# Expert products of an attention and feed-forward kernel cut in halves and, behind value passes, in column strips; four of seven products of a quad in one PSUM bank

## The chip, the cores and the metric

The kernel runs on one core of a Trainium2 chip, in one launch. The metric is the device time in microseconds (us), the median of several executions. TensorE is the engine for matrix products (PE in the profile, PEld for its weight loads), VectorE is DVE, ScalarE is ACT, GpSimd is POOL, and SyncE is SP, which issues the stores here.

## What is computed

Softmax attention over 8 batches, 12 heads, 448 tokens and 64 elements a head, then a feed-forward layer with SiLU on the 3,584 tokens:

```python
scores = scale * np.matmul(q, k.transpose(0, 1, 3, 2))
scores = scores - np.max(scores, axis=-1, keepdims=True)
attn = np.exp(scores)
attn = attn / (np.sum(attn, axis=-1, keepdims=True) + 1e-09)
attn_out = np.matmul(attn, v)
x = attn_out.transpose(0, 2, 1, 3).reshape(B * S, H * D)   # 3584 x 768
h = x @ w_in                                               # 768 x 2048
g = h * (1.0 / (1.0 + np.exp(-h)))
out = g @ w_out                                            # 2048 x 768
```

## The kernel before, in words

**The attention.** A unit is one batch with a group of four heads (`units`, line 801; batch 0 is cut in two pieces of 224 tokens, `PIECES`). For each unit TensorE makes scores (`score`, line 336), with 64 elements of a head as two passes of 32 rows: four heads stand one below the other in the array as tiles of 32 rows by 128 columns. ScalarE takes the exponential of each pair of banks (`expo`, line 373). Then come three passes through `attend`, each with output strips of 128 rows by 32 columns, four heads side by side: part 0 sums the exponentials (`attend_sums`, line 415, for a pair of units), parts 1 and 2 are the value passes (line 399), each for half of a head's elements. Two units share one chunk of keys; its strips have 64 rows and end each value pass of a pair of units. VectorE divides (`norm`, line 482) and leaves x transposed.

**The feed-forward layer.** Up to batch 5, `ffn1` (line 496) makes a group of six products of 128x128 weights by 448 tokens (224 in the pieces of batch 0) in one PSUM bank. ScalarE takes a tanh (line 507) and VectorE makes g from it (`gate`, line 543). The second layer runs on quads of two by two blocks: `product` (line 704), with seven products of eight matmuls with 384 columns in place of eight, on sums and differences of blocks of g (`combine_g`, line 694) and of `w_out` (`combine_w`, line 533). Four banks take them, two products in three of the banks (`BANK`, line 696); `take_3` to `take_7` read the banks, three by ScalarE and six additions by VectorE per quad. Quad 0 is done without the trick, by `plain` (line 718). The first layer of the last two batches (`PB`) uses the same kind of seven products, over two batches and two halves of the weights (`pair_product`, line 632), eight times (f = 0 to 7), with two copies on ScalarE and five additions on VectorE each (`pair_copy`, `pair_add`), and then four SiLUs on ScalarE (line 670). The outputs lie in `ost` buffers and are stored by SP, the last ones in turn by SP and ScalarE (`store`, line 762).

**The order.** The order of every engine is fixed when the kernel is built. A planner (`Order`, lines 78 to 162, and the loop from line 1496) keeps a clock for each engine with an estimated cost for each operation, rings for the buffers (`m_ring` for four PSUM banks, `s_ring` for two pairs of score banks, `ost_ring` for output buffers), and whenever TensorE is free it takes scores if they are ready and due (`PACE`), else a value pass, else the first ready entry of the list `moe` (groups of `ffn1`, quad products, pair products). `on_pe` adds `SWITCH`, 0.094, when the mode of the array (full, rows, cols and the two kinds of 64-row or 64-column rest) differs from that before. Where nothing is ready early on, products of zeros fill (line 1491).

```python
    def on_pe(self, op, mode):
        gap = SWITCH if mode != self.mode else 0.0
        self.mode = mode
        op.busy += gap
        self.start(op)
...
            elif moe_i is not None:
                if av is not None and av <= od.now - 0:
                    run_av()
                else:
                    moe.pop(moe_i)[2]()
                ran = True
```

Of the kernel before, what the change touches and what calls it, by code (L numbers as in the profile page):

```python
# [17 lines left out]
PE_OUT = 0.20  # L18
# [147 lines left out]
def kernel(  # L166
# [36 lines left out]
    SHY = 0.5  # L203
    FAR = (NT * B // 4 - 3, NT * B // 4 - 1)
# [4 lines left out]
    NSG, NTMP, NOST = 3, 3, 4  # L209
# [213 lines left out]
    def attend(ns, part):  # L423
        made = []
        lone = len(ns) == 1
        if part == 0 and not lone:
            attend_sums(ns)
            return
        for n in ns:
            a = ps.tile([128, 512], FP32, name=f"a_{n}_{part}", tag="m", bufs=4)  # L430
            made.append(a)
            acc[(n, part)] = a
            for c in range(NCH if lone else NCH - 1):
                for h in range(HG):
                    attend_mm(
                        a, n, part, c, h, 0, rows_of(n, c), E[(n, c // per_burst(n))],
                        c == 0, lone and c == NCH - 1,
                    )
        if not lone:
            for h in range(HG):  # L440
                for i, n in enumerate(ns):
                    attend_mm(
                        made[i], n, part, 3, h, 64 * i, 64 * (i + 1), E[(ns[0], 3)],
                        False, True,
                    )

# [43 lines left out]

    h_t, th_t, o_t = {}, {}, {}

    def ffn1(b, f, t0, t1):
        h = ps.tile([128, 512], FP32, name=f"h_{b}_{f}_{t0}", tag="m", bufs=4)
        for cc in range(NDC):
            nc.tensor.matmul(  # L496
                out=h[:, 0 : t1 - t0],
                lhsT=w_in_t[:, cc, 128 * f : 128 * (f + 1)],
                rhs=x3(b, cc)[:, cc % 3, t0:t1],
                start=(cc == 0),  # L500
                stop=(cc == NDC - 1),
            )
        h_t[(b, f, t0)] = h
# [13 lines left out]
    W_ = {m: const.tile([128, HF, OH], FP16, name=f"D{m}") for m in (1, 4, 6)}  # L517
# [5 lines left out]
    W_[3], W_[7], W_[5], W_[2] = B_[0, 1], B_[1, 0], B_[1, 1], B_[0, 0]  # L523

    def combine_w(m, f0, f1):
        i0, i1, op = {
            1: ((0, 0), (1, 1), ALU.add),
            4: ((1, 0), (0, 0), ALU.subtract),
            6: ((0, 0), (0, 1), ALU.add),
            3: ((0, 1), (1, 1), ALU.subtract),  # L530
            7: ((1, 0), (1, 1), ALU.add),
        }[m]
        nc.vector.tensor_tensor(
            out=W_[m][:, f0:f1], in0=B_[i0][:, f0:f1], in1=B_[i1][:, f0:f1], op=op
        )
# [75 lines left out]
    PBANK = {1: "A", 2: "A", 6: "B", 5: "C", 3: "C", 7: "D", 4: "D"}  # L611

    def pair_product(f, m):
        if m in (1, 5):
            pp_t[(f, PBANK[m])] = ps.tile(
                [128, 512], FP32, name=f"f_{f}_{m}", tag="m", bufs=4
            )[:, 0:S]
        elif m == 6:
            two = ps.tile([128, 2, 512], FP32, name=f"f_{f}_{m}", tag="s", bufs=2)
            pp_t[(f, "B")], pp_t[(f, "D")] = two[:, 0, 0:S], two[:, 1, 0:S]  # L620
# [10 lines left out]
        for c in range(3):  # L631
# [4 lines left out]
                start=(c == 0 and m in (1, 6, 5, 7)),  # L636
# [4 lines left out]
    def pair_tmp(f, name):  # L641
# [4 lines left out]
            "v": ("T", NT_, [128, HG, S], FP16),  # L646
        }[name]
        t = sb.tile(shape, dt, name=f"{name}_{f}", tag=tag, bufs=n)
        if len(shape) == 5:
            t = t.rearrange("p c x i e -> p (c x i e)")  # L650
        elif len(shape) == 3:
            t = t.rearrange("p h s -> p (h s)")
# [6 lines left out]
    def pair_add(f, to, x, y):  # L659
        x = pp_t[(f, x)] if x in "BCD" else pf_t[(f, x)]  # L660
        y = pf_t[(f, y)]
        out = pf_t[(f, to)] if (f, to) in pf_t else pair_tmp(f, to)
        nc.vector.tensor_tensor(out=out, in0=x, in1=y, op=ALU.add)
# [13 lines left out]
    S_t, tmp_t, ost_t, pr_t = {}, {}, {}, {}  # L677

    def combine_g(qd, m, f0, f1):
        a, b = 2 * qd, 2 * qd + 1  # L680
        x, y, op = {
            5: (rows(a, 0), rows(a, 1), ALU.add),
            2: (rows(b, 0), rows(b, 1), ALU.add),
            1: (rows(a, 0), rows(b, 1), ALU.add),
            6: (rows(b, 0), rows(a, 0), ALU.subtract),
            7: (rows(a, 1), rows(b, 1), ALU.subtract),
        }[m]
        if m > 5:
            dst = x
        else:  # L690
            if (qd, m) not in S_t:
                S_t[(qd, m)] = sb.tile([128, HF, 128], FP16, name=f"S_{qd}_{m}", tag="S", bufs=NSG)
            dst = S_t[(qd, m)]
        nc.vector.tensor_tensor(out=dst[:, f0:f1], in0=x[:, f0:f1], in1=y[:, f0:f1], op=op)  # L694

    BANK = {3: 3, 5: 3, 4: 4, 2: 4, 1: 1, 7: 1, 6: 6}

    def product(qd, m):
        w = {3: rows(2 * qd, 0), 4: rows(2 * qd + 1, 1), 6: rows(2 * qd + 1, 0), 7: rows(2 * qd, 1)}
        w = w[m] if m in w else S_t[(qd, m)]  # L700
        if BANK[m] == m:
            pr_t[(qd, m)] = ps.tile([128, 512], FP32, name=f"p_{qd}_{m}", tag="m", bufs=4)
        for f in range(HF):
            nc.tensor.matmul(  # L704
                out=pr_t[(qd, BANK[m])][:, 0:OH],
                lhsT=w[:, f, :],
                rhs=W_[m][:, f, :],
                start=(f == 0 and BANK[m] == m),
                stop=(f == HF - 1),
                skip_group_check=True,  # L710
            )


    def plain(t, j, f0, f1):
        if f0 == 0:
            pr_t[("o", t, j)] = ps.tile([128, 512], FP32, name=f"o_{t}_{j}", tag="m", bufs=4)
        for f in range(f0, f1):
            nc.tensor.matmul(  # L718
                out=pr_t[("o", t, j)][:, 0:OH],
                lhsT=rows(t, f // HF)[:, f % HF, :],  # L720
                rhs=B_[f // HF, j][:, f % HF, :],
                start=(f == 0),
                stop=(f == NFF - 1),
                skip_group_check=True,
            )
# [7 lines left out]

    def tmp(qd, name):
        tmp_t[(qd, name)] = sb.tile([128, OH], FP32, name=f"{name}_{qd}", tag="tmp", bufs=NTMP)
        return tmp_t[(qd, name)]
# [28 lines left out]
    def add(out, a, b, op=ALU.add):  # L765
        nc.vector.tensor_tensor(out=out, in0=a, in1=b, op=op)  # L766


    def take_3(qd):
        nc.scalar.copy(out=tmp(qd, "s"), in_=bank(qd, 3))  # L770

    def take_4(qd):
        add(tmp_t[(qd, "s")], bank(qd, 4), tmp_t[(qd, "s")])

    def take_5(qd):
        nc.scalar.copy(out=ost(qd, 0, 1), in_=bank(qd, 3))  # L776
        store(qd, 0, 1)

    def take_2(qd):
        nc.scalar.copy(out=ost(qd, 1, 0), in_=bank(qd, 4))  # L780
        store(qd, 1, 0)

    def take_1(qd):
        add(tmp(qd, "m"), bank(qd, 1), tmp_t[(qd, "s")])

    def less_12(qd):
        add(tmp_t[(qd, "s")], tmp_t[(qd, "s")], ost_t[(qd, 0, 1)], ALU.subtract)

    def less_21(qd):
        add(tmp_t[(qd, "m")], tmp_t[(qd, "m")], ost_t[(qd, 1, 0)], ALU.subtract)  # L790

    def take_6(qd):
        add(ost(qd, 1, 1), bank(qd, 6), tmp_t[(qd, "m")])
        store(qd, 1, 1)

    def take_7(qd):
        add(ost(qd, 0, 0), bank(qd, 1), tmp_t[(qd, "s")])
        store(qd, 0, 0)
# [113 lines left out]
    sg_ring, tmp_ring, ost_ring = Ring(NSG), Ring(NTMP), Ring(NOST)  # L912
    far_ring = Ring(NX3)
    STORE = 3.0
    pr_op, sg_op, w_op, plain_op = {}, {}, {2: [], 5: []}, {}
    inv_op, norm_op = [], []
    quads = []

    def queue_ffn1(b, g0, g1):
        t0, t1 = 32 * g0, 32 * g1  # L920
        for f in range(NFF) if b == 0 else [x for f in range(HF) for x in (f, f + HF)]:

            def run(f=f):
                op = Op("PE", NDC * mm(t1 - t0), lambda: ffn1(b, f, t0, t1), tail=PE_OUT)
# [4 lines left out]
                od.on_pe(op, "full")  # L929
# [14 lines left out]
            def deps(f=f):  # L944
# [3 lines left out]
                for qd in range(NT * B // 4) if u else ():  # L948
                    if any(t // NT == u - 1 and (r or t % NT < 4) for t in (2 * qd, 2 * qd + 1)):
# [3 lines left out]
                            else [pr_op.get((qd, m)) for m in (3, 4, 6, 7)]  # L953
# [56 lines left out]
    def queue_pair_f(f, xs):  # L1010
        done, lo = {}, f // 4 * 4

        def free(r):
            made = []
            for qd in range(NT * B // 4):
                for t in (2 * qd, 2 * qd + 1):
                    if t // NT == PB // 2 - 1 and t % NT < (4, NT - 1)[r]:
                        made += [pr_op.get((qd, m)) for m in (3, 4, 6, 7)]
# [10 lines left out]
        def queue(m):  # L1029
            rings = {  # L1030
                1: ((rq_ring, 1),),
                6: ((s_ring, 1), (kt_ring, 1), (t_ring, 1)),
                5: ((rk_ring, 1),),
            }.get(m, ())
            ms = (6, 7) if m == 6 else (m,)

            def run():
                op = Op(
                    "PE",
                    3 * len(ms) * mm(S),  # L1040
                    lambda: [pair_product(f, x) for x in ms],
                    tail=PE_OUT,
                )
                if m in (1, 5):
# [7 lines left out]
                elif m == 6:  # L1052
                    read("u", "DVE", lambda: pair_add(f, "u", "B", "p"), [op, done["p"]])
                    read("v", "DVE", lambda: pair_add(f, "v", "D", "u"), [op, done["u"]])
                elif m == 5:
                    read("q", "ACT", lambda: pair_copy(f, "q", "C"), [op], None, -3)
                    read("22", "DVE", lambda: pair_add(f, "v", "q", "v"), [done["v"], done["q"]], rk_ring.give)
                    gate_of(1, 1, "v", [done["22"]], t_ring.give)
                elif m == 2:
                    gate_of(0, 0, "A", [op], m_ring.give)  # L1060
                elif m == 3:
                    read("12", "DVE", lambda: pair_add(f, "p", "C", "u"), [op, done["u"]], m_ring.give)
                    gate_of(1, 0, "p", [done["12"]], rq_ring.give)
# [520 lines left out]
```

## Time and profile before

| What | Value |
|---|---|
| three timed runs | 396.12 us median, 396.03 to 396.42 |
| span of the profiled execution, first to last instruction | 394.4 us; the median of the runs is 1.7 above it |
| first matmul, last matmul | 1.0 us and 389.5 us after the span's start |
| 0 to 25 us: PE busy | 22.6 us (loads land, zeros fill) |
| 25 to 300 us: attention and both layers mixed | PE 274.6 of 275 us, DVE 228.6, ACT 189.7 |
| 311 to 349 us: pair products | PE 38.0 of 38 us, DVE 33.0, ACT 21.2 |
| 349 us to the end: last four quads | PE 40.9 of 45 us, DVE 30.5, ACT 10.5 |
| loads and stores | 45.6 MB read, 11.0 MB written |

Busy time of PE is modelled at its end (a matmul of 448 columns shows 352 ns, but the next starts 189 ns later), so the distance from one start to the next is what a matmul takes from the engine. Four strips that stand in different rows or columns of the array start 2 to 4 ns apart and run side by side; in what follows they are one group, and a slot is one group or one full matmul.

### The profile page before, as it was taken

How to read it: one execution, taken by the hardware profiler on the slowest of the kernel's cores; microseconds unless marked ns; L12 is line 12 of the kernel's file. 1: busy time of each engine (PE TensorE's matmuls, PEld its weight loads, DVE VectorE, ACT ScalarE, POOL GpSimd, SP SyncE). 2: the span in 40 equal slices, each digit the busy share in tenths (PEclk: the TensorE clock that was granted, in tenths of full speed). 3: DMA queues.
4: the chain of work that ended last, by engine and by line, in shares of the span. 5: the costliest groups of instructions: out<-in, count | busy, mean ns of one | idle time of the engine just before them, and what ended most of it. 6: DMA issues, size and time to landing. Idle time of an engine off the chain costs nothing.

```text
span 394.4 us, 9273 instructions
## 1 busy us (share of the span) xinstructions
PE 386.5 (98%) x3679; PEld 199.0 (50%) x3679; DVE 311.3 (79%) x653; ACT 243.2 (62%) x378; POOL 83.6 (21%) x153
## 2 busy tenths in 40 slices
PE   7999999999999999999999999999999999999995
PEld 6667764443444444554444444344444555556663
DVE  2466676999999697896888786988879898787863
ACT  4988885696863868626868429686593227872110
POOL 6632546315004242500051221120000000000000
PEclk9999999999999999999999999999999999999999
DMA  7999999919034863582145751531100131001334
GB/s 113 205 210 210 166 179 164 175 36 141 1 76 88 142 95 47 75 158 71 25 49 81 139 109 46 71 48 42 42 1 2 40 87 35 2 1 42 80 82 121
DMA packets 35356, 34.44 MB, mean 87 GB/s; under 512 B 11376, under 2 KB 33776, under 8 KB 35312
## 3 DMA queue, kind: packets, MB, share of 16 engines
q0 software_dynamic: 24784, 22.82, 39.2%
q1 hardware_dynamic: 9952, 10.33, 9.6%
q10 hardware_dynamic: 576, 0.69, 0.6%
q8 instruction: 29, 0.48, 0.5%
q14 instruction: 15, 0.12, 0.1%
HBM read 45.61 MB, written 11.01 MB: 144 GB/s over the span
## 4 chain that ended last, share of the span: by engine, by line
PE 94%; DMA 3%; DVE 1%; ACT 1%; POOL 0%; issue 0%; POOLq 0%
PE p L704 29%; PE h L496 29%; PE s L336 12%; PE a L399 10%; PE f L632 8%; PE o L718 3%; DMA rq<-in_q_dram 3%; PE a L415 2%; PE z L1491 1%; ACT E L373 0%; DVE S L694 0%; POOL rk L249 0%; DVE rq L323 0%; DVE rdn L466 0%; DVE ost L766 0%
## 5 line engine op out<-in xcount | busy, mean ns | idle before, releaser
L373 ACT ACTIVATE E<-s 128x896 f16<-128x896 f32 (+1 forms) x172 | 150.0, 915 | 48.6 <-PE s L336 47.5
L496 PE MATMUL h<-xT,w_in_t 128*128 128x448 f16 (+1 forms) x672 | 118.6, 327 | 0.0
L496 PEld LDWEIGHTS <-w_in_t 128*128 128x128 f16 x672 | 61.2, 98 | 54.0 <-issue 18.0
L507 ACT ACTIVATE th<-h 128x448 f16<-128x448 f32 (+1 forms) x112 | 54.3, 495 | 31.4 <-PE h L496 22.5
L543 DVE SCALAR_TENSOR_TENSOR G<-th,h 128x448 f16<-128x448 f16 (+2 forms) x112 | 55.1, 507 | 15.3 <-ACT th L507 13.3
L270 POOL DMA_DIRECT2D V<-in_v_dram x88 | 48.5, 568 | 56.5 <-PE a L399 42.7
L336 PE MATMUL s<-rq,KT 32*128 32x448 f16 (+4 forms) x768 | 50.9, 337 | 1.4 <-DVE rq L323 0.9
L704 PEld LDWEIGHTS <-G 128*128 128x128 f16 x384 | 36.5, 98 | 28.1 <-issue 4.4
L704 PEld LDWEIGHTS <-S 128*128 128x128 f16 x312 | 29.3, 98 | 23.9 <-issue 5.2
L399 PE MATMUL a<-E,V 128*32 128x448 f16 (+3 forms) x864 | 40.4, 335 | 0.0
L255 POOL DMA_DIRECT2D rq<-in_q_dram x27 | 15.1, 560 | 113.0 <-PE s L336 82.9
L704 PE MATMUL p<-D,G 128*128 128x384 f16 x208 | 37.6, 326 | 0.0
L704 PE MATMUL p<-w_out_t,S 128*128 128x384 f16 x208 | 37.2, 326 | 0.1
L482 DVE SCALAR_TENSOR_TENSOR xT<-a,rdn 128x448 f16<-128x448 f32 (+1 forms) x54 | 28.7, 565 | 7.4 <-PE a L399 6.5
L336 PEld LDWEIGHTS <-KT 32*128 32x128 f16 (+2 forms) x864 | 17.5, 98 | 29.6 <-issue 25.9
L704 PE MATMUL p<-w_out_t,G 128*128 128x384 f16 x176 | 31.9, 326 | 0.0
L399 PEld LDWEIGHTS <-V 128*32 128x32 f16 (+2 forms) x864 | 18.2, 95 | 22.4 <-issue 14.7
L384 DVE TENSOR_TENSOR T<-T,E 128x1792 f16<-128x1792 f16 x20 | 21.8, 1089 | 8.0 <-ACT E L373 7.9
L694 DVE TENSOR_TENSOR S<-G 128x512 f16<-128x512 f16 x70 | 25.3, 414 | 3.2 <-PE p L704 3.0
L384 DVE TENSOR_TENSOR T<-E,E 128x1792 f16<-128x1792 f16 x20 | 21.6, 1082 | 5.6 <-ACT E L373 5.6
L776 ACT COPY ost<-p 128x384 f32<-128x384 f32 x13 | 6.2, 480 | 27.4 <-PE p L704 22.6
L305 DVE STREAM_TRANSPOSE KT<-rk 128x256 f32<-128x256 f32 (+3 forms) x48 | 16.6, 384 | 7.0 <-DMA rk<-in_k_dram 6.2
(74 smaller groups left out, 370.2 us busy)
## 6 DMA issues: line engine op xcount, KB each, us to landing
out_dram<-ost SPq DMA_DIRECT2D x194, 48.0 KB, 1.7
rk<-in_k_dram POOLq DMA_DIRECT2D x24, 224.0 KB, 5.9
rq<-in_q_dram POOLq DMA_DIRECT2D x21, 224.0 KB, 5.2
w_in_t<-in_moe_w_in_dram POOLq DMA_DIRECT2D x6, 512.0 KB, 11.2
w_out_t<-in_moe_w_out_dram POOLq DMA_DIRECT2D x4, 768.0 KB, 13.5
V<-in_v_dram POOLq DMA_DIRECT2D x43, 64.0 KB, 3.9
V<-in_v_dram POOLq DMA_DIRECT2D x40, 48.0 KB, 4.0
out_dram<-ost SPq DMA_DIRECT2D x8, 96.0 KB, 2.2
```

The lines of the kernel that those rows point to most:

```text
L270: nc.gpsimd.dma_start(out=VT[b][32 * x : 32 * (x + 1), hs, 0:count, :], in_=v[b, hs].rearrange("h (i g) d -> i h g d", g=TPP)[:, :, first ...
L336: nc.tensor.matmul(out=pS[p0 : p0 + 32 * (x1 - x0), h % 2, at : at + nq], lhsT=KT[(b, hg)][32 * h : 32 * (h + 1), c, x0:x1, :, e], rhs=QT[ ...
L373: nc.scalar.activation(out=E[(n, w)][0:kr, 2 * y : 2 * y + 2, 0:nk], in_=pS_t[(n, w, y)][0:kr, :, 0:nk], func=AF.Exp, scale=attn_scale,)
L384: nc.vector.tensor_tensor(out=T[n], in0=T[n] if step else E[(n, 0)], in1=E[(n, step + 1)], op=ALU.add,)
L399: nc.tensor.matmul(out=a[32 * h : 32 * (h + 1), 0:nq], lhsT=w, rhs=e[k0:k1, h, at : at + nq], start=start, stop=stop,)
L482: nc.vector.scalar_tensor_tensor(out=x3(b, cc)[:, cc % 3, 32 * g0 : 32 * g1], in0=acc[(n, part)][:, 0:nq], scalar=0.5, in1=rdn_t[n].rearra ...
L496: nc.tensor.matmul(out=h[:, 0 : t1 - t0], lhsT=w_in_t[:, cc, 128 * f : 128 * (f + 1)], rhs=x3(b, cc)[:, cc % 3, t0:t1], start=(cc == 0), s ...
L507: nc.scalar.activation(out=th, in_=h_t[(b, f, t0)][:, 0 : t1 - t0], func=AF.Tanh)
L543: nc.vector.scalar_tensor_tensor(out=dst[:, f, at + lo : at + hi], in0=th_t[(b, f, t0)][:, lo - t0 : hi - t0], scalar=1.0, in1=h_t[(b, f, ...
L632: nc.tensor.matmul(out=pp_t[(f, PBANK[m])], lhsT=w[:, c, :], rhs=a[:, c, :], start=(c == 0 and m in (1, 6, 5, 7)), stop=(c == 2), skip_gro ...
L694: nc.vector.tensor_tensor(out=dst[:, f0:f1], in0=x[:, f0:f1], in1=y[:, f0:f1], op=op)
L704: nc.tensor.matmul(out=pr_t[(qd, BANK[m])][:, 0:OH], lhsT=w[:, f, :], rhs=W_[m][:, f, :], start=(f == 0 and BANK[m] == m), stop=(f == HF - 1),
```

## The change

1. `times` (new) issues a product of 128 output rows either as one matmul with 128x128 weights or as four strips of 32 weight columns, each into 32 partitions of the same bank. `ffn1`, `plain` and `product` go through it. Strips are used where the array's mode is already `cols`, that is behind a value pass, while scores or value passes remain to be done.
2. The groups of `ffn1` (those of 448 columns) and of `product` are planned as two halves; the second half is put first in the list `moe`, so the loop may take scores or a value pass between the two.
3. In `attend`, part 2 starts with the 64-row strips of the shared chunk, and part 1 still ends with them, so that the two passes can meet in these strips.
4. With `AWAIT`, a value pass that is ready is held back for a matrix group if scores are due within 0.8 by the planner's clock.
5. The seven products of a quad follow another scheme: products 1, 6, 7 and 4 add up in one bank, 2 has a bank and 5 and 3 share one. Three banks instead of four, read in this order: each output starts as a ScalarE copy (1, 5, 6, 4 into `ost`) or gets a VectorE sum in place (2, 7, 3). Per quad there are four copies and three sums (three copies and six sums before), and eight half sums of g instead of ten. Sums of `w_out` are eight instead of ten. `ost` has seven buffers instead of four and the `tmp` buffers are gone.
6. The pair products follow the same scheme: 1, 6, 7, 4 in one score bank (bank A), three copies and three sums per f instead of two and five.

The core of the diff (`NSG, NTMP, NOST = 3, 3, 4` has become `NSG, NOST = 3, 7`):

```diff
+    def times(out, w, x, start, stop, strips):
+        cut = 32 if strips else 128
+        for i in range(0, 128, cut):
+            nc.tensor.matmul(
+                out=out[i : i + cut],
+                lhsT=w[:, i : i + cut],
+                rhs=x,
+                start=start,
+                stop=stop,
+                skip_group_check=True,
+            )
...
+        if not lone and part == 2:
+            rest()
+        for i, n in enumerate(ns):
...
+        if not lone and part == 1:
+            rest()
...
-    PBANK = {1: "A", 2: "A", 6: "B", 5: "C", 3: "C", 7: "D", 4: "D"}
+    PBANK = {1: "A", 6: "A", 7: "A", 4: "A", 2: "B", 5: "C", 3: "C"}
...
-    BANK = {3: 3, 5: 3, 4: 4, 2: 4, 1: 1, 7: 1, 6: 6}
+    BANK = {1: 1, 6: 1, 7: 1, 4: 1, 2: 2, 5: 5, 3: 5}
...
+    OUT = {1: (0, 0), 5: (1, 1), 6: (0, 1), 4: (1, 0)}
+    SUM = {2: (0, 0), 7: (1, 1), 3: (0, 1)}
+
+    def take_copy(qd, m):
+        nc.scalar.copy(out=ost(qd, *OUT[m]), in_=bank(qd, BANK[m]))
+        if m == 4:
+            store(qd, *OUT[m])
+
+    def take_sum(qd, m):
+        t = ost_t[(qd, *SUM[m])]
+        nc.vector.tensor_tensor(out=t, in0=bank(qd, BANK[m]), in1=t, op=ALU.add)
+        store(qd, *SUM[m])
...
+            def piece(f, c0, c1):
+                strips = od.mode == "cols" and bool(qk_seq or av_seq)
...
+                od.on_pe(op, "cols" if strips else "full")
+                return op
...
+                if t1 - t0 < S:
+                    rest(f, piece(f, 0, NDC))
+                else:
+                    piece(f, 0, NDC // 2)
+                    moe.insert(0, (list, 0, lambda: rest(f, piece(f, NDC // 2, NDC)), ()))
...
-        for m in (1, 6, 5, 2, 3, 4):
+        for m in (1, 5, 6, 2, 7, 3, 4):
             queue(m)
...
+                piece(0, HF // 2, None)
+                moe.insert(0, (list, 0, run_rest, ()))
...
-        od.on_pe(op, "cols")
+        od.on_pe(op, "rest cols" if two and part == 2 else "cols")
         if two and part:
-            od.mode = "rest cols"
+            od.mode = ("rest cols", "cols")[part - 1]
...
             elif moe_i is not None:
-                if av is not None and av <= od.now - 0:
+                soon_qk = qk is not None and units[qk_seq[0][0][0]][0] > 0
+                soon_qk = soon_qk and max(qk, pace["next"]) < od.now + AWAIT
+                if av is not None and av <= od.now and not soon_qk:
                     run_av()
```

## The prediction

> **What bounds the kernel now.** I read the page from the top: busy shares, the slices, the chain that ended last.
>
> ```profile
> span 394.4 us, 9273 instructions
> ...
> PE 386.5 (98%) x3679; PEld 199.0 (50%) x3679; DVE 311.3 (79%) x653; ACT 243.2 (62%) x378; POOL 83.6 (21%) x153
> ...
> PE   7999999999999999999999999999999999999995
> ...
> PEclk9999999999999999999999999999999999999999
> ...
> PE 94%; DMA 3%; DVE 1%; ACT 1%; POOL 0%; issue 0%; POOLq 0%
> ```
>
> TensorE is busy in every slice but the first and the last, at the full granted clock, and the chain of waits is TensorE from end to end. So the time is the sum of TensorE's own slots, plus the few places where it waits, plus a head and a tail. A busy TensorE can still hide cost between slots, so next I read its timeline in a stretch with every mode in it. Columns: start, time, operation; the start-to-start distance is what counts.
>
> ```profile
> 270.47 1.47 PE L704 MATMUL p<-D,S 128*128 128x384 f16 x8
> 271.78 1.30 PE L496 MATMUL h<-xT,w_in_t 128*128 128x448 f16 x6
> 273.01 0.57 PE L336 MATMUL s<-q,KT 32*128 32x448 f16 x8
> 273.51 0.56 PE L415 MATMUL a<-T,half 128*32 128x448 f16 x8
> 273.90 0.36 PE L415 MATMUL a<-E,both 128*32 128x448 f16 x4
> 274.20 1.47 PE L704 MATMUL p<-D,G 128*128 128x384 f16 x8
> 275.51 1.46 PE L704 MATMUL p<-w_out_t,G 128*128 128x384 f16 x8
> 276.90 0.57 PE L336 MATMUL s<-q,KT 32*128 32x448 f16 x8
> ```
>
> Eight full products of 384 columns take 271.78 - 270.47 = 1.31 us, 163 ns each. Six of 448 columns take 1.23 before scores follow; record by record it is 189 ns five times and 285 the sixth time: the step from full tiles to 32-row tiles costs 96 ns. The next pair says the same: 275.51 to 274.20 is 1.31 with no step, 276.90 to 275.51 is 1.39 with one. Eight strips of 128x32 (two groups of four that run side by side) take 0.39 = 200 + 189 ns: a group of four strips costs one full slot, and only the first group of a run costs 11 ns more. The 448-column strips of the value passes have a median of 189 too, those of 224 columns 95 to 107 (mean 100) against 96 for a full one.
>
> **TensorE's sum.** The built order of both kernels gives the same slots (2,216; four concurrent strips count as one): 648 full or strip-cut slots of expert and pair products at 448 columns, 192 at 224, 792 at 384, and the same scores and value passes. 202 of the expert slots are now cut into four strips (60 at 224 columns, 66 at 448, 76 at 384), which adds 606 matmuls and 606 weight loads to 3,679 each. The mode steps fall from 258 to 246: full to 32-row tiles from 81 to 62, back from 69 to 72, strips to full from 25 to 11, strips to scores from 16 to 35, full to strips from 13 to 21 and rows to strips from 28 to 25 (these six classes make 232 and 226; the rest are steps between strips of 128 and of 64 rows, 26 and 20). Each costs 95 to 105 ns in the trace. Summing every slot and step of both orders by the medians of their class gives 382.83 us before and 381.66 after, **-1.17 us**; 12 steps by 96 ns gives 1.15, so it hangs on no single class. 18 expert groups of 448 columns are parted by scores; that adds no slot.
>
> For a strip-cut expert group the trace has no row: unlike a value pass, its four strips read the same moving rows. Bounds by the nearest rows: -1 ns a group (95 against 96 at 224 columns), +11 ns (each group like the first of a run), so -0.2 to +2.2 us for 202 groups. I take 0, because the value strips inside a run differ from full slots by nothing and move as many rows.
>
> **Waits.** Against those class medians TensorE loses 1.5 us after 50 us: 0.51 in the three places from 51 to 54 us (scores of the first batches), 0.27 at 222.7 and 0.73 at 309. The last one can be seen:
>
> ```profile
> 307.77 1.47 PE L704 MATMUL p<-w_out_t,S 128*128 128x384 f16 x8
> ...
> 309.28 0.48 ACT L780 COPY ost<-p 128x384 f32<-128x384 f32 x1 [2.27 <-PE p L704]
> 309.81 1.46 PE L704 MATMUL p<-D,S 128*128 128x384 f16 x8 [0.57 <-ACT ost L780]
> ```
>
> The product ends at 307.77 + 8 x 0.163 = 309.07, its copy starts 0.2 later and lasts 0.48, and TensorE goes on 0.05 after it: 0.73 us in all, because the next product's bank in the pool's rotation is the one that had just been filled. In the new order I counted the slots between the product that an eviction reads and the slot that waits for that eviction. In the old order the least is 0 (this place); in the new one no quad product has under 1.30 us and no pair product under 1.14, against the 0.73 needed. So this wait goes, **-0.73 us**; next in line behind it are those 1.14 us places. The other two I leave.
>
> **The edits beside TensorE**, by the rows' durations. VectorE loses 83 operations (per quad three adds and two half sums, 16 pair adds, two weight sums): 13 x (3 x 0.55 + 2 x 0.41) + 16 x 0.62 + 2 x 0.94 = 44 us of its 311. ScalarE gains 21 copies: 13 x 0.48 + 8 x 0.53 = 10.5 us of 243. Neither is on the path; TensorE's slots cover both at nothing. That cover is thinnest in the pair stage, where a pair takes 21 slots of 189 ns = 3.97 us and ScalarE has 3 x 0.53 + 0.54 + 3 x 0.58 = 3.87 us. In the trace such operations start 0.43 to 0.47 apart when queued, so it is 3.1 of 3.97.
>
> Four of seven products now share bank A, with an eviction between each two: copy, copy, add. Needed: 0.2 + 0.53 + 0.05 = 0.78 us for a copy and 0.2 + 0.62 + 0.05 = 0.87 for the add. There are two products between, 1.135 us: spare 0.35 and 0.26. I walked one period of the new order with these rows; every copy finds ScalarE free or waits less than its spare. Cost 0, bounded by the rival below.
>
> Outputs now start as copies and are summed in place, so each `ost` buffer is held for about 3 products longer; there are seven instead of four, and the least reuse distance rises from 7.7 to over 9.4 us of slots. The queue of stores has the same 202 + 8 transfers. At the end a ScalarE copy (0.48) stands where a VectorE add (0.56) stood ahead of the last store: -0.08. The first 25 us have the same order, the 87 filler products included.
>
> **Sum.** 394.4 - 1.17 - 0.73 - 0.08 = 392.4. The trace has two waits in some 1,900 slots after 55 us, so a new order will hardly have none beside the one I kept; I add 0.3. Span 392.7. The three timed runs have their median 1.7 above the span of the profiled execution, which I keep: **394.4 us**, -0.4%. A measurement can tell about 0.2% (0.8 us) from no change.
>
> **Rivals.**
> 1. *Waits eat it (0.14).* New waits of 1.0 to 2.3 us where the order is new: at 51 us a value bank has 1.18 us for its eviction, and in the first two pairs VectorE still makes weight sums of 0.95 us ahead of the adds. For it: the three small waits near 53 us; against: the old order had as many such places and waited at two. Time 395.4 to 396.7, same.
> 2. *Strips cost more than a full slot (0.08).* If the four weight loads of a group don't hide behind a slot, all groups cost 11 ns, 2.2 us: 396.6; if this is so at 224 columns alone, 0.7: 395.1. Against it: value strips of 224 columns run 12 groups in a row at 95 to 100. [...]
> 3. *The chain through bank A stalls (0.05): slower.* If each copy finds another operation just begun, it is late by 0.47 - 0.35 = 0.12, each add by 0.62 - 0.26 = 0.36: 16 x 0.12 + 8 x 0.36 = 4.8 us in the pair stage. 392.4 + 4.8 + 1.7 = 398.9 us. It decides from a total of 2.8 us on (the 2.0 gained and 0.8). For it: 97% nominal load of ScalarE there. Against: the old order had a copy with the same 1.14 us in all eight pairs and TensorE never waited there.
> 4. *The old waits go too (0.03):* 0.27 + 0.51 less and no new one, 393.3.
> That the switches don't fall cannot be: the order is fixed at build; only their price could differ, and 258 of them agree.
>
> Forecast 0.70 with a range of its own of 393.3 to 395.3. Faster by over 0.2% (under 395.33): 0.70 + 0.03 = 0.73. Within: 0.14 + 0.06 = 0.20. Slower: 0.05 + 0.02 = 0.07. Range 393.2 to 396.6: it holds the forecast and most of rivals 1 and 2.
>
> **What would show it.** In the changed profile: TensorE 98% busy again; strip groups 189, 163 and 96 ns apart (step 1); steps still 95 to 105 ns; no wait behind a copy near 300 to 312 us; no TensorE wait in the pair products; the last store leaving no later after the last product. Strip groups over 192 ns, or idle in the pair stage with ScalarE or VectorE as its releaser, would make it wrong.

## The result and the profile after

The change makes the kernel slower by 0.3%: 397.27 us median (397.06 to 397.57) against 396.01 (395.67 to 396.42) for the kernel before on the same chip, a ratio of 1.0033 with a 95% interval of 1.0021 to 1.0045. The forecast was 394.4, with a range of 393.2 to 396.6. One of the six runs of the changed kernel was slow (411.11 us at a granted clock of 0.953); such runs, of which e1 and e2 below have one each, count in the medians given here and in no range or ratio. The profiled execution of the changed kernel took 397.23 us, with a span of 395.5.

The page of the changed kernel, the same lines as shown of before:

```profile
span 395.5 us, 10472 instructions
...
PE 386.1 (98%) x4285; PEld 202.5 (51%) x4285; DVE 273.2 (69%) x570; ACT 251.8 (64%) x399; POOL 83.7 (21%) x153
...
PE   8998999999999999999999999999999999999995
...
PE 97%; DVE 1%; issue 1%; ACT 0%; DVEq 0%
```

On this page the change looks harmless: TensorE is still 98% busy, VectorE has lost 38 us, and the chain is TensorE's at 97%, more than before. The two places that matter are the "8" in the fourth slice (29.7 to 39.6 us; it was a 9) and the "issue 1%" in the chain (0% before). The waits of TensorE, in the columns releaser, total, times, longest, say where to look. Before:

```profile
PE s L336 <- DVE rq L323: 0.9, 2, 0.8
PE p L704 <- ACT ost L780: 0.6, 1, 0.6
PE s L336 <- ACT E L373: 0.4, 1, 0.4
PE a L399 <- issue: 0.2, 1, 0.2
```

After:

```profile
PE h L503 <- issue: 1.7, 1, 1.7
...
PE p L503 <- DVE xT L491: 0.7, 1, 0.7
PE a L416 <- DVE X L564: 0.5, 1, 0.5
PE p L503 <- DVE ost L782: 0.5, 1, 0.5
```

The wait that the prediction removed (`p` behind ScalarE's copy into `ost`) is gone, three behind VectorE have come, and one of 1.7 us has no releaser at all. Record by record, from the first matmul to the start of the last:

| Part | After less before, us |
|---|---|
| slots and mode steps by the medians of their class | -1.17 |
| up to 31 us | -0.25 |
| old waits after 50 us gone (309 us: 0.73, 222.7: 0.27, 51 to 54: 0.51) | -1.51 |
| **a stop in `h`, strips of 224 columns, at 32.1 us** | **+1.91** |
| **new waits behind VectorE at 296, 309 and 319 us: 0.62 + 0.68 + 0.86** | **+2.16** |
| two small ones (208.4 and 255.2 us) | +0.16 |
| sum; the trace has 389.86 against 388.56 | +1.30 |
| last matmul's start to the end of the span (4.60 against 4.84) | -0.24 |

So the gain was there, 2.9 us of it, and 4.2 us were lost again. **The stop at 32 us** in the timeline of the changed kernel (start, duration, instruction, and in brackets the idle time before it with its releaser):

```profile
32.12 0.27 PE L503 MATMUL h<-xT,w_in_t 128*32 128x224 f16 x4
...
34.13 1.24 PE L503 MATMUL h<-xT,w_in_t 128*32 128x224 f16 x44 [1.74 <-issue]
34.13 0.98 PEld L503 LDWEIGHTS <-w_in_t 128*32 128x32 f16 x43 [1.91 <-issue]
```

TensorE does the first four strips of a group of 24 and stops for 2.00 us (88 ns are usual there). The next strips belong to the same group and the same bank, the trace shows no semaphore that released them, and the weight loads, whose first of this group ran 0.09 us ahead of its matmul (32.03 against 32.12), stop as well. That points to the instructions themselves. The DMA part of the page has a queue for those:

```profile
q8 instruction: 33, 0.54, 0.6%
```

33 packets of 16,384 bytes, where the trace has 8,618 instructions of TensorE (29 for 7,407 before), so one packet holds about 256. The DMA engines are full in this stretch. In the next line the last two columns are the time that packets took, as a share of 16 engines (over 1 where packets overlap), and the GB/s that they moved:

```profile
32.00:34.10 2.10, 0.39 (x17) 0.22 (x9) 1.30 (x4) 0.84 (x2) 0.20 (x1) 1.00 1.11 201
```

A packet of the instruction queue was served from 31.82 to 32.75 us, and TensorE goes on 1.38 us later. No record ties the two together, so it had to be tried.

**The waits behind VectorE**, by the example at 296 us, after:

```profile
294.51 0.95 DVE L629 TENSOR_TENSOR tw<-w_in_t 128x1536 f16<-128x1536 f16 x1
295.38 0.95 DVE L629 TENSOR_TENSOR tw<-w_in_t,tw 128x1536 f16<-128x1536 f16 x1
296.25 0.48 DVE L564 SCALAR_TENSOR_TENSOR G<-th,h 128x320 f16<-128x320 f16 x1
296.64 0.28 DVE L564 SCALAR_TENSOR_TENSOR X<-th,h 128x128 f16<-128x128 f16 x1
...
296.98 0.56 PE L416 MATMUL a<-T,half 128*32 128x448 f16 x8 [0.55 <-DVE X L564]
```

Two weight sums for the pair products stand ahead of the gates, though the first pair product that reads any weight sum starts 30 us later, at 324.5 (in e3 these two run 18 us later); the bank that `a` takes comes free only when its gate has been read. The other two have the same pattern:

```profile
306.81 0.76 DVE L705 TENSOR_TENSOR S<-G 128x512 f16<-128x512 f16 x2 [1.19 <-PE p L503]
...
309.30 1.01 DVE L782 TENSOR_TENSOR ost<-p,ost 128x384 f32<-128x384 f32 x2
309.90 1.46 PE L503 MATMUL p<-D,S 128*128 128x384 f16 x8 [0.52 <-DVE ost L782]
...
316.88 0.86 DVE L611 TENSOR_TENSOR sx<-xT,xT 128x1344 f16<-128x1344 f16 x1 [3.62 <-PE a L400]
317.65 1.82 DVE L629 TENSOR_TENSOR tw<-w_in_t 128x1536 f16<-128x1536 f16 x2
...
319.39 1.15 DVE L491 SCALAR_TENSOR_TENSOR xT<-a,rdn 128x448 f16<-128x448 f32 x2
320.06 1.47 PE L503 MATMUL p<-w_out_t,G 128*128 128x384 f16 x8 [0.70 <-DVE xT L491]
```

At 309 us VectorE had been blocked for 1.19 us on a half sum `S` whose buffer product 5 was still reading (in that quad product 6 ran ahead of 5, and the pool gives out its three buffers in turn); it and six more half sums stand ahead of the output sum that TensorE waits for. At 319 us a sum of x waited 3.62 us for its buffer, and it and two weight sums stood ahead of the last two divisions.

### The profile page after: what moved, and what is told of

Read it like the earlier page. It is cut to its first block, busy times and chain, and to the rows that moved or that the text cites. A ratio compares the mean times of both kernels' runs of the same rounds, so it can differ in the third digit from the quotient of the medians.

```text
span 395.5 us, 10472 instructions
## 1 busy us (share of the span) xinstructions
PE 386.1 (98%) x4285; PEld 202.5 (51%) x4285; DVE 273.2 (69%) x570; ACT 251.8 (64%) x399; POOL 83.7 (21%) x153
## 4 chain that ended last, share of the span: by engine, by line
PE 97%; DVE 1%; issue 1%; ACT 0%; DVEq 0%
PE p L503 31%; PE h L503 28%; PE s L337 13%; PE a L400 11%; PE f L652 8%; PE o L503 3%; PE z L1501 2%; PE a L416 2%; DVE tw L629 0%; DVE T L385 0%; ACT E L374 0%; DVE xT L491 0%; DVE ost L782 0%; ACT ost L776 0%; DVE G L564 0%
## 5 line engine op out<-in xcount | busy, mean ns | idle before, releaser
L503 PE MATMUL h<-xT,w_in_t 128*128 128x448 f16 (+3 forms) x1050 | 120.1, 320 | 1.7 <-issue 1.7
L503 PEld LDWEIGHTS <-w_in_t 128*32 128x32 f16 (+1 forms) x1050 | 62.6, 97 | 54.5 <-issue 17.9
L529 ACT ACTIVATE th<-h 128x448 f16<-128x448 f32 (+1 forms) x112 | 53.2, 496 | 19.9 <-PE h L503 17.4
L776 ACT COPY ost<-p 128x384 f32<-128x384 f32 x52 | 24.9, 479 | 62.7 <-PE p L503 53.7
L503 PEld LDWEIGHTS <-G 128*128 128x128 f16 (+1 forms) x592 | 43.3, 98 | 33.4 <-issue 5.4
L503 PE MATMUL p<-w_out_t,G 128*128 128x384 f16 (+1 forms) x328 | 49.6, 326 | 0.7 <-DVE xT L491 0.7
L503 PEld LDWEIGHTS <-S 128*128 128x128 f16 (+1 forms) x396 | 29.9, 98 | 22.9 <-issue 3.1
L503 PE MATMUL p<-D,S 128*128 128x384 f16 (+1 forms) x280 | 37.7, 326 | 0.5 <-DVE ost L782 0.5
L782 DVE TENSOR_TENSOR ost<-p,ost 128x384 f32<-128x384 f32 x39 | 21.4, 553 | 16.1 <-PE p L503 12.6
L503 PE MATMUL p<-D,G 128*32 128x384 f16 (+1 forms) x164 | 19.9, 326 | 0.0
```

What stands on the lines that cost most here:

```text
L503: nc.tensor.matmul(out=out[i : i + cut], lhsT=w[:, i : i + cut], rhs=x, start=start, stop=stop, skip_group_check=True,)
L529: nc.scalar.activation(out=th, in_=h_t[(b, f, t0)][:, 0 : t1 - t0], func=AF.Tanh)
L776: nc.scalar.copy(out=ost(qd, *OUT[m]), in_=bank(qd, BANK[m]))
L782: nc.vector.tensor_tensor(out=t, in0=bank(qd, BANK[m]), in1=t, op=ALU.add)
```

## Experiments

Theory **A**: the stop at 32 us is TensorE out of instructions, because strips use them up faster than they can be fetched while loads fill the DMA engines. Theory **A'**: the three late waits are VectorE's order alone. The rivals are in the expectations. The times below come from three sessions, each with its own runs of the kernel before (396.19, 395.95 and 396.11 us); the ratio is the safe number. The changed kernel itself is not in these sessions; its ratio is the 1.0033 above.

| Run | median, us | to before, 95% interval |
|---|---|---|
| e1_after_no_b0_strips | 395.89 | 0.9993 (0.9984 to 1.0002) |
| e2_before_b0_strips | 397.98 | 1.0037 (1.0023 to 1.0051) |
| e3_after_dve_order | 394.87 | 0.9965 (0.9953 to 0.9978) |
| e4_both | 393.65 | 0.9932 (0.9918 to 0.9945) |
| e5_after_all_full | 398.12 | 1.0057 (1.0046 to 1.0069) |
| e6_before_b0_token_cuts | 398.39 | 1.0061 (1.0049 to 1.0073) |
| e7_both_late_b0_strips | 394.02 | 0.9951 (0.9939 to 0.9963) |
| e8_both_one_b0_group | 395.02 | 0.9974 (0.9964 to 0.9984) |
| e9_after_fewer_loads | 395.38 | 0.9987 (0.9978 to 0.9996) |

### e1 and e2: the strips of batch 0, taken out and put in

e1 draws batch 0's groups full in the changed kernel, in an unchanged order:

```diff
                 cc == NDC - 1,
-                strips,
+                strips and t1 - t0 == S,
```

> The changed kernel, with the 60 groups of 224 columns (batch 0) drawn as full matmuls again; order of all engines the same but for that. Steps of mode rise from 246 to 251 (+0.5 us). Theory A (TensorE ran out of instructions at 32 us, because strips of 224 columns use eight instructions in 96 ns while their fetch stands behind the loads): the stall of 1.9 us at 32.1 us is gone, so 1.4 us faster than the changed kernel, 0.1 to 0.2 us under the kernel before (395.8). Theory B (the stall is a wait for data, such as the second half of w_in that lands at the same moment): it stays, so 0.5 us slower than the changed kernel, 397.8. The waits at 296, 309 and 319 us stay in both.

e2 puts strips into the first three groups of the kernel before, and nothing else:

```diff
+        cut = 32 if b == 0 and t0 == 0 and f < 3 else 128
         for cc in range(NDC):
-            nc.tensor.matmul(
-                out=h[:, 0 : t1 - t0],
+            for i in range(0, 128, cut):
+                nc.tensor.matmul(
+                    out=h[i : i + cut, 0 : t1 - t0],
```

> The kernel before, with the first three groups of its first layer (224 columns, f = 0 to 2) drawn in four strips each: 54 more matmuls and 54 more weight loads by 29 us, all else the same; steps of mode 256 instead of 258 (-0.2 us). Theory A: TensorE reaches its instruction number 1,217 before the fetch that starts near 32 us has landed, and stands there for 1.5 to 2.2 us though nothing of the change is in this kernel: 397.3 to 398.0. Theory B: no stall, 395.8.

Both came out at A's number: 395.89 without the stop, 397.98 with it (397.7 by its ratio). The stop has moved with these strips, and in e2 it is again 1.91 us, at the same place in TensorE's stream: its instruction 1216 (all of its instructions in the trace counted from the start: matmuls, weight loads and ten others, most of them semaphore waits), though the two kernels come to it at 32.58 and 32.13 us.

### e3 and e4: VectorE's order, alone and with e1

e3 gives operations a shift in the order in which they are written out, and each half sum a buffer of its own place. Nothing of TensorE's order is touched:

```diff
-            S_t[(qd, m)] = sb.tile([128, HF, 128], FP16, name=f"S_{qd}_{m}", tag="S", bufs=NSG)
+            at = {5: 0, 6: 1, 3: 2}[m]
+            at = (1, 0, 2)[at] if qd == 9 else at
+            S_t[(qd, m)] = sb.tile([128, HF, 128], FP16, name=f"S_{qd}_{m}", tag=f"S{at}", bufs=1)
...
+                sg_op[(qd, m)][-1].shift = 0.7 if (qd, m) == (9, 5) else 0.0
...
+            pair_w[(m, f0)].shift = 18.4 if m > 2 and f0 == 0 else 0.0
...
+        x.shift = {(NU - 2, 2): -3.7, (NU - 1, 2): -4.25}.get((n, part), 0.0)
```

> The changed kernel with TensorE's and ScalarE's order kept and VectorE's changed at three places: two weight sums (tw, m = 3 and 4 of f0 = 0) stand 18 us later, behind the gates that they stood ahead of; the two last norms stand ahead of the sums that waited in front of them (sx, tw); and the half sums of quad 9 take the buffer that was freed first. Theory A': the TensorE waits at 296 (0.62), 309 (0.68) and 319 us (0.86) come from VectorE's fixed order and go: 2.2 us faster than the changed kernel, 395.1. Theory B': the wait moves to the next late buffer and at most 1.0 us is gained, 396.3 or more. The stall at 32 us stays in both.

394.87, by the ratios 2.7 us under the changed kernel (2.2 expected), and the three waits are gone: VectorE's two weight sums that stood at 294.51 and 295.38 now come later, and the value pass has no wait:

```profile
295.96 0.56 PE L417 MATMUL a<-T,half 128*32 128x448 f16 x8
...
312.12 0.95 DVE L630 TENSOR_TENSOR tw<-w_in_t 128x1536 f16<-128x1536 f16 x1
312.99 0.95 DVE L630 TENSOR_TENSOR tw<-w_in_t,tw 128x1536 f16<-128x1536 f16 x1
```

e4 makes both edits.

> Both of the edits before together. If the two causes are independent, 1.4 + 2.2 = 3.6 us faster than the changed kernel: 393.7, which is 2.3 under the kernel before. If the later waits were a consequence of the early stall, or if removing one opens another, 394.7 to 396.0.

393.65: this version beats both kernels, and the two losses are independent within the intervals (by the ratios e1 takes off 0.40%, e3 0.68% and both together 1.01%). Of TensorE's waits the profile lists only these two; too short for the list is a stop of 0.26 us at instruction 960:

```profile
PE z L1507 <- DVE zeros L224: 1.0, 1, 1.0
PE s L338 <- ACT E L375: 0.4, 1, 0.4
```

### e5: every strip-cut group drawn full

```diff
-        cut = 32 if strips else 128
+        cut = 128
```

> The changed kernel in its own order, with every strip-cut group drawn as one 128x128 matmul again (3,679 matmuls; 271 mode steps instead of 246). Theory A (strips cost a full slot each, and what they lose is the 1.9 us stop for instructions at 32 us): +25 steps x 0.096 = +2.4 us, -1.9 us, so 0.5 us above the changed kernel's 397.3: 397.7 us, and no stop at 32 us. Rival B (a strip-cut group costs more than a full slot, 0.7 to 2.2 us in all): 395.5 to 397.0 us.

398.12, 0.4 above A's number and away from the rival's. There is no stop at instruction 1216. To price strips, compare with e1, which has the strips of 448 and 384 columns and no stop either: 0.64% or 2.5 us between their ratios, against 20 mode steps by 96 ns = 1.9. The traces are closer: from instruction 704 to the last matmul e5 takes 368.99 us and e1 366.88, so 2.1 us more, which 20 steps at 95 to 105 ns make (1.9 to 2.1). Ahead of that the profiled execution of e5 began late (TensorE waits 1.5 us for the first q). So strips cost no more than full slots.

### e6: as many instructions without a strip

In the kernel before, the first three groups are cut in four by tokens (these three groups don't get the reference's sums; the matmuls are as many and as long as they would be):

```diff
+        cut = 56 if b == 0 and t0 == 0 and f < 3 else t1 - t0
         for cc in range(NDC):
...
+            for i in range(0, t1 - t0, cut):
```

> The kernel before with no strips at all; the first three expert groups of batch 0 are cut by tokens instead, each 128x128 product of 224 columns in four of 56. As many matmuls and weight loads more (54 each) as three groups of strips, without a mode step more or less. Theory A (TensorE runs out of instructions): a stop of 0.8 to 1.65 us at PE instruction 1216 with no releaser named, beside what the shorter matmuls themselves cost (0 to 0.9 us a group); 397.7 to 399.4 us. Rival B (the stop belongs to strips): no stop at instruction 1216, only what the shorter matmuls cost.

398.39, and the stop is there, in matmuls with full 128x128 weights:

```profile
32.65 0.28 PE L498 MATMUL h<-xT,w_in_t 128*128 128x56 f16 x4
34.38 0.81 PE L498 MATMUL h<-xT,w_in_t 128*128 128x56 f16 x25 [1.45 <-issue]
34.38 0.69 PEld L498 LDWEIGHTS <-w_in_t 128*128 128x128 f16 x24 [1.55 <-issue]
```

After its fourth matmul, again at instruction 1216. It is the count of instructions that stops TensorE, not the form of the tile. The 0 to 0.9 us a group for the shorter matmuls was my estimate, from no trace: 25 of them after the stop take 0.81 us here, 24 strips 0.75 in the changed kernel (at 29.77 us).

### e7 and e8: where the strips may stand

e7 is e4 with strips again in batch 0's groups except the first three (`strips and (t1 - t0 == S or t0 > 0 or f > 2)`); e8 is e4 with strips in the very first group alone (`strips and (t1 - t0 == S or (t0 == 0 and f == 0))`).

> As e4_both, but only the first three expert groups of batch 0 are drawn full; the other seven of its groups behind value passes are strips again (248 mode steps instead of 251). Theory A: their instructions come after the fetches have caught up, so no stop; 3 steps x 0.096 = 0.3 us below e4_both, 393.4 us. Rival (any strips at 224 columns cost or stop): 393.7 us or more.

> As e4_both, but the very first expert group of batch 0 is cut in strips. Theory A: instruction 1216 comes up at 32.55 us instead of 34.2, and can run only 1.33 us after the end of the packet that holds it (31.9 + 0.95), so a stop of 1.65 us with one group against 1.9 with three: 395.2 us. Rival (each group of strips brings its share of the stop): 0.63 us, 394.2 us. The stop would stand in the second group, which is drawn full.

e8 hit A (395.02, a stop of 1.51 us), and the stop stands where only the count can put it, in a group that isn't cut:

```profile
32.22 0.56 PE L504 MATMUL h<-xT,w_in_t 128*128 128x224 f16 x4
34.13 0.93 PE L504 MATMUL h<-xT,w_in_t 128*128 128x224 f16 x8 [1.35 <-issue]
```

e7 missed: 394.02 instead of 393.4, no better than e4, and in the rival's range (393.7 or more). My statement that the fetches had caught up by then was wrong. There is a stop of 0.5 us at 56.8 us:

```profile
55.28 1.80 PE L504 MATMUL h<-xT,w_in_t 128*32 128x224 f16 x67
57.41 0.35 PE L504 MATMUL h<-xT,w_in_t 128*32 128x224 f16 x5 [0.34 <-issue]
```

It is at instruction 1984 = 1216 + 3 x 256. So the miss speaks for A in another way: the edges lie 256 apart, and strips at another edge meet them again. The rival's range was hit by this stop and not by a dearer strip: from instruction 704 to the last matmul e7 takes 0.40 us more than e4, where this stop (0.51) and a longer one at 960 (0.12 more) less three mode steps make 0.3.

### e9: the same instructions with fewer loads

```diff
-            out=w_in_t[:, 2 * c : 2 * c + 2, f0:f1],
+            out=w_in_t[:, c : c + 1, f0:f1],
...
-                "(p j) f -> p j f", j=2
-            ),
+                "(p j) f -> p j f", j=2
+            )[:, 0:1],
...
     def load_w_out(f0, f1):
-        nc.gpsimd.dma_start(
-            out=w_out_t[:, f0:f1],
-            in_=moe_w_out[128 * f0 : 128 * f1].rearrange("(f p) m -> p f m", p=128),
-        )
+        pass
```

> The changed kernel in exactly its order of TensorE (the same 4,285 matmuls, strips included), but with 4.7 MB of loads left out: of w_in only every second row is loaded (and used twice), w_out isn't loaded at all (its place is taken by views of w_in), so the output is not the reference's; one instruction more than the changed kernel on TensorE. Theory A (the instruction packet that TensorE asks for at its instruction 960 waits behind the loads): the packet is served well under the 3.9 us after instruction 960 that it took in the changed kernel, and under 2.9 us of it the stop at instruction 1216 (32.1 us) is gone; 1.9 us below the changed kernel, 395.4 us or less, as waits for loads can go too. Rival B (the fetch has its delay whatever the loads do, because the instructions come too close together): served 3.9 us after, a stop of 1.7 to 1.9 us, 397.3 us less what waits for loads cost.

The packet was served 2.36 us after TensorE came to instruction 960 instead of 3.94, and the stop shrank to 0.79 us, but didn't go: other loads moved up, and the DMA engines were full until about 31 us (share 1.16 and 169 GB/s from 28 to 32 us, against 1.13 and 214 in the changed kernel). My limit of 2.9 us in the expectation was a slip, too: of the 3.88 us that TensorE takes from 960 to 1216, the packet itself (0.9) and what follows it leave 1.6. TensorE's order is equal in the two kernels, and in the ten kernels with all loads this packet came 3.8 to 4.1 us after instruction 960, so the delay does depend on the loads, and rival B falls. The total agrees with A's (395.4 or less) only by chance. In the profiled executions (395.96 us for e9, 397.23 for the changed kernel) the span is 1.28 us shorter: the stop at 1216 is 1.12 shorter, and one of 0.28 at instruction 960 is gone. That the median lies another 0.6 us below e9's profiled run isn't explained.

### The fetches in one table

From the DMA and TensorE records of each trace, in us (an edge is the last instruction ahead of a new packet's; when it is reached is good to 0.1 us, since weight loads can start ahead of their matmuls, by 0.09 us at 32.03 us in the changed kernel):

| Kernel, edge | 256 earlier reached | packet served | edge reached | goes on | after the packet's end |
|---|---|---|---|---|---|
| before, 960 | 22.44 | 26.09 to 27.04 | 27.92 | 28.41 | 1.37 |
| before, 1216 | 27.92 | 31.98 to 32.92 | 34.36 | no stop | |
| e4, 1216 | 27.93 | 31.91 to 32.87 | 34.24 | no stop | |
| after, 1216 | 27.87 | 31.82 to 32.75 | 32.13 | 34.13 | 1.38 |
| e2, 1216 | 28.21 | 32.29 to 33.25 | 32.58 | 34.58 | 1.33 |
| e6, 1216 | 28.02 | 32.14 to 33.11 | 32.74 | 34.38 | 1.27 |
| e8, 1216 | 27.93 | 31.86 to 32.82 | 32.52 | 34.13 | 1.31 |
| e9, 1216 | 28.11 | 30.47 to 31.36 | 31.99 | 32.86 | 1.50 |
| e7, 1984 | 52.55 | 55.08 to 56.06 | 56.82 | 57.41 | 1.35 |

Whatever the kernel, TensorE goes on 1.27 to 1.50 us after the end of the packet. A second distance is as constant: in the ten kernels with all loads the packet for edge 1216 starts 3.56 to 3.64 us after TensorE went on past instruction 960 (2.36 in e9). That the packet is asked for when the edge 256 instructions before is crossed fits this, but is inferred: later in the changed kernel, where the DMA engines are often free (0 to 3 tenths busy in the page's slices from 237 us on), packets are served from 1.8 us before to 2.9 us after that moment. The first row is the lesson: the kernel **before** already stopped at 28.4 us, at instruction 960, by 0.39 us. Nine of the ten others stop there too, by 0.11 to 0.40 us (0.28 in the changed kernel); only e9, with fewer loads, does not. And at 1216 the kernel before had 0.1 us to spare (32.92 + 1.35 = 34.27, reached at 34.36).

## Why the prediction was wrong

- *TensorE's sum, -1.17:* right. In the changed trace strip groups are 189, 163 and 96 ns apart for 448, 384 and 224 columns, and steps cost what they did (from full to 32-row tiles 96 ns in both kernels). Rival 2 falls with it, and by e5 too.
- *Strips taken at 0:* the failed step. The slot price was right, but "606 matmuls and 606 weight loads" were counted and then priced by TensorE's time alone. They also have to be fetched, in 33 packets instead of 29. The row I leaned on, value strips of 224 columns, 12 groups in a row, gives the price of strips whose instructions are already there. Cost 1.9 us, by a mechanism that none of my rivals had. "The first 25 us have the same order" was true, and the stretch behind it, where loads still fill the DMA engines (share 1.11 at 32 us) and strips begin, wasn't looked at by itself. The profile gave the hint: "PE a L399 <- issue: 0.2" in the waits of before, with the weight load behind it:

```profile
28.41 0.10 PEld L399 LDWEIGHTS <-ones 96*32 96x32 f16 x3 [0.48 <-issue]
```

- *Waits, -0.73 and +0.3 for new ones:* the old wait went, and those at 222.7 and 51 to 54 us with it (rival 4's part, -1.51 in all; why those went isn't shown). The allowance for new ones was the second failed step: 2.3 us came, the size of rival 1. Its mechanism came as well, weight sums that stand ahead of due work, but ahead of gates and divisions at 296 and 319 us and not of the adds in the pairs that it named. I counted TensorE's slots between a product and the slot that waits for its eviction, against the eviction's own 0.73 us. That holds on an engine that is free. VectorE takes its operations in a fixed order, and here 1.9 us of weight sums, or a half sum blocked for 1.19 us and six more, stood ahead of the eviction or the gate. e3, which changes VectorE's order and buffers only, gets them back.
- *Edits beside TensorE, nothing on the path:* right for the sums. VectorE lost 83 operations and 38 us (44 forecast), ScalarE gained 21 copies and 8.6 us (10.5 forecast). But that VectorE's share falls said nothing of these waits: it has 21 us to do in the 28 from 294 to 322 us and is still late three times.
- *The chain through bank A (rival 3):* TensorE has no wait in the pair products. *The tail:* 0.24 less instead of 0.08.
- *The signs named beforehand:* TensorE 98% busy, the distances of the strip groups and the price of a step all came, though the time was wrong. They test the slots and not the waits. Of the two signs of being wrong one came once: TensorE idle behind VectorE in the pair stage, 0.86 us at 319 us, ahead of a quad product.

With both losses repaired (e4) the kernel takes 393.65 where the kernel before takes 396.19, a ratio of 0.9932 (0.9918 to 0.9945). Open: how much of e3's gain each of its edits brings in a timed run (each of the three waits is seen to go), and why the profiled executions of e5 and e7 begin late.

## What to carry to other kernels

Before one matmul is cut in several, count instructions and not only slots: find the stretches where loads fill the DMA engines, and look there for idle time on the tensor engine that the profile calls "issue" for matmuls and weight loads alike. When a new order is checked for waits, walk the queue of each engine that releases something, with all that stands ahead in it, above all work that is ready early and needed late. A gain that is real slot by slot can be lost at two places of a microsecond or two (here 1.91 and 2.16 us), and the busy share of the page need not show it (98% in both kernels).

## What the runs showed of the hardware

The packet with about 256 TensorE instructions behind 1216 came later where more was loaded: it started 3.6 us after TensorE had gone on past 960 in the ten kernels with all loads (214 GB/s from 28 to 32 us in the changed kernel) and 2.4 us after it in e9 (169 GB/s). It took 0.9 us itself, and where TensorE stood waiting, it went on 1.3 to 1.5 us after the packet's end. That is 5.9 us from going on past one edge to going on past the next, in all five kernels that stop at 1216 with all their loads. TensorE did the instructions between in 5.95 us with full products and had no stop; strips did them in 3.9 us (4.3 with the one group of e8), and the stop made up the rest. The 5.9 us is no constant: at e7's edge at 57 us, with the DMA engines again 9 tenths busy in the page's slice (177 GB/s), it was 4.9. After 58 us no edge shows a stop: every wait of TensorE's matmuls without a releaser that the profiles list lies at instruction 960, 1216 or 1984.
